# Attention plus gated MLP on one core: visits of the attention at other places, and the last output block stored in two halves

## The chip, the cores and the metric

The kernel runs on one core of one Trainium2 chip. The metric is the device time of one execution in microseconds (us), lower is better. A core has the engines PE (TensorE, matrix products into PSUM banks), DVE (VectorE), ACT (ScalarE), POOL (GpSimd) and SP (SyncE). Each runs its own list of instructions in order and waits on semaphores for the others. SP, ACT and POOL also issue DMAs.

## The reference

Local attention over 8 batches, 8 heads, 576 tokens and head size 64, then a gated MLP over all 4608 tokens (512 to 1536 to 512), in float32:

```python
def _attn_ref(q, k, v):                       # (8, 8, 576, 64)
    scores = scale * np.matmul(q, k.transpose(0, 1, 3, 2))
    mask_plain = (rel >= 0) & (rel < 32)                       # heads 0 to 3
    mask_dil = (rel >= 0) & (rel < 128) & (rel % 4 == 0)       # heads 4 to 7
    scores = np.where(masks[None, :, :, :], scores, -1000000000.0)
    attn = np.exp(scores - np.max(scores, axis=-1, keepdims=True))
    attn = attn / (np.sum(attn, axis=-1, keepdims=True) + 1e-09)
    return np.matmul(attn, v)

def _moe_ref(x, w_gate, w_val, w_out):        # x: the attention's output, (4608, 512)
    g = x @ w_gate
    silu = g * (1.0 / (1.0 + np.exp(-g)))
    return silu * (x @ w_val) @ w_out
```

## The kernel before

**Tokens.** The first 1536 tokens are worked off in four plain chunks of 384, the other 3072 in three chunks of 1024 (`NCS` = 3, each two halves of `CS` = 512 columns). The change touches the 1024-token chunks, called chunk 0, 1 and 2 here.

**Products.** Every float32 operand of the MLP is split into a high and a low part, and three products (high by high, high by low, low by high) are added in PSUM (L772). A 1024-token chunk multiplies by seven products in place of eight: operands are cut into 2 by 2 blocks, `NT` = 7 combinations of blocks are multiplied, and sums of the products give the four blocks of the result. Product t goes to a pair of PSUM banks (`BANK`): bg/bv for products 0, 2 and 4 (ACT copies them out, `keep`, L777), bo0/bo1 for 1 and 5, bo2/bo3 for 3 and 6. After products 1, 4, 5 and 6 DVE adds a bank and a kept copy (`total`, L735). The totals of product 4 read bo2/bo3, which product 6 then adds to, so product 6 has to wait for them.

**Two stages of a chunk.** In the gate/value stage six rounds (i = 0 to 5, pairs of hidden blocks) each run the seven products, each once for the gate and once for the value (`gate_val`): 84 slots of six matmuls. After each total `gated` forms tanh (ACT, L798) and the gated h (DVE, L800, L801). In the second stage (the output, `outs`) each of the seven products runs over six hidden blocks: 42 slots, each with three matmuls for either of two row blocks r. Its operands are h and combinations of h (DVE, POOL), split by `h_split` (ACT cast L762, then the low part on DVE or POOL, L735) eight blocks ahead. Where a product is in `SUMS`, `out_done` forms the total of a row block and SP stores it (256 KB). So a chunk has 126 slots, 0 to 83 gate/value and 84 to 125 output; the change of stages lies behind slot 83. Weights come as pieces that POOL asks for seven ahead (`ask`, L701).

**Attention.** It is cut into 46 packs. While chunk c is multiplied, PE, DVE and ACT also do the attention of chunk c + 1, in ten visits for each of chunks 0 and 1; chunk 2 has none. A visit m has two parts, hung behind a slot by the dictionary `visit` (`attend`). Part A at slot a: PE forms the results of pack m - 1 (L394) and the scores of pack m (L354); DVE divides (L403 to L405) and subtracts the row maximum (L366 to L369); ACT takes exponentials (L374) and issues two loads (L336, L330). Part B, six slots later: PE transposes the results (L412) and the exponentials (L378); ACT copies both out (L384, L438). All use the one pair of banks `two`. Before, the ten parts A of a chunk stood at slots 2, 12, 22, 32, 42, 53, 63, 73, 83 and 94.

**x.** When a chunk's attention is complete, `x_step` forms the seven combinations of the next chunk's x and splits them (ACT cast L738, DVE L735, both 1024 columns). In the program most steps stand at slots 104 to 124, but the compiler's scheduler may put a step earlier in an engine's list where its data allow it.

## Time and profile before

| | |
|---|---|
| median of 3 runs | 946.74 us (946.68 to 948.36) |
| the profiled execution | 946.37 us, of it the span of the instructions 944.6 us |
| granted TensorE clock | 1.000 |
| busy share of the span: DVE, ACT, POOL | 67%, 41%, 37% |
| memory | 161.37 MB read, 42.47 MB written, 216 GB/s |

A row of the timeline has the start in us, the duration, the engine, the source line, the operation, output and inputs, and a count of like instructions; in brackets stands how long the engine was idle before it and what ended that. A row of a waits table reads: who waited, on which line, for whom; the sum in us, how often, the longest. "at_..." is an SBUF buffer, "two", "bg", "bv", "bo" are PSUM banks. ACTq and SPq are the queues from which DMAs are issued.

### The profile page before, as it was taken

What the parts mean: (1) busy time and instruction counts of PE and PEld (TensorE: products, weight loads), DVE (VectorE), ACT (ScalarE), POOL (GpSimd) and SP (SyncE); (2) the same over time, 40 slices, a digit from 0 to 9 for tenths busy, and PEclk for the clock granted to TensorE, in tenths of its full rate; (3) what the DMA queues carried; (4) which work ended last, traced back from release to release, by engine and by line L of the source; (5) the groups of instructions that cost most, each with busy time, mean ns of one, the idle gap of its engine ahead of it and who ended that gap; (6) DMA issues with size and microseconds to landing.
All of it is one profiled execution on the core that took longest, in us unless ns stands there. A gap on an engine that the chain in (4) does not pass through costs nothing.

```text
span 944.6 us, 21916 instructions
## 1 busy us (share of the span) xinstructions
PE 929.7 (98%) x9204; PEld 812.9 (86%) x9204; DVE 633.3 (67%) x1008; ACT 391.9 (41%) x687; POOL 346.1 (37%) x364
## 2 busy tenths in 40 slices
PE   7899999999999999999999999999999999999998
PEld 5799999999999999888888788888887888888886
DVE  4767566676667865666568984666689845656882
ACT  4885323333234333343344553343345523334352
POOL 0765411111111121234245672232257723344481
PEclk9999999999999999999999999999999999999999
DMA  9986166567757690777768688776865786665583
GB/s 369 336 283 199 36 206 222 175 228 236 242 189 248 234 332 31 234 239 209 226 203 255 210 240 257 225 235 202 253 203 166 226 261 191 201 183 176 176 252 105
DMA packets 75249, 205.25 MB, mean 217 GB/s; under 512 B 7568, under 2 KB 23824, under 8 KB 75152
## 3 DMA queue, kind: packets, MB, share of 16 engines
q0 software_dynamic: 27216, 99.10, 34.9%
q1 hardware_dynamic: 35696, 65.07, 19.5%
q10 hardware_dynamic: 12240, 39.70, 12.7%
q8 instruction: 72, 1.18, 0.5%
q14 instruction: 25, 0.20, 0.1%
HBM read 161.37 MB, written 42.47 MB: 216 GB/s over the span
## 4 chain that ended last, share of the span: by engine, by line
PE 91%; DVE 5%; ACT 2%; issue 1%; DMA 0%; ACTq 0%; DVEq 0%
PE bo L772 30%; PE bg L772 11%; PE bv L772 11%; PE bo L496 10%; PE bv L459 10%; PE bg L459 10%; PE two L394 3%; PE two L354 2%; PE two L378 2%; DVE at_float L735 2%; PE two L412 1%; DVE at_int L263 0%; DMA at_bfloat<-masks 0%; DVE at_float L800 0%; DVE at_float L801 0%
## 5 line engine op out<-in xcount | busy, mean ns | idle before, releaser
L772 PE MATMUL bo<-at_float32r 128*128 128x512 f32 x1296 | 308.0, 391 | 0.0
L772 PEld LDWEIGHTS bo<-at_float32r 128*128 128x128 f32 x1296 | 242.1, 188 | 51.6 <-ACT at_float L503 0.2
L701 POOL DMA_DIRECT2D at_float32r<-pieces x189 | 103.9, 550 | 249.5 <-PE bo L772 144.5
L735 DVE TENSOR_TENSOR at_float<-bo,at_float 128x512 f32<-128x512 f32 x168 | 113.7, 685 | 109.8 <-ACT at_float L777 59.8
L488 POOL TENSOR_TENSOR at_float32r<-at_float,at_float32r 128x384 fp32r<-128x384 f32 x48 | 54.9, 1143 | 220.0 <-PE bo L496 180.0
L772 PE MATMUL bv<-at_float32r 128*128 128x512 f32 x486 | 129.9, 393 | 0.0
L772 PE MATMUL bg<-at_float32r 128*128 128x512 f32 x486 | 129.7, 393 | 0.0
L735 DVE TENSOR_TENSOR at_float32r<-at_float,at_float32r 128x512 fp32r<-128x512 f32 (+1 forms) x84 | 99.2, 1205 | 40.3 <-ACT at_float32r L762 24.8
L735 POOL TENSOR_TENSOR at_float32r<-at_float,at_float32r 128x512 fp32r<-128x512 f32 x63 | 96.7, 1536 | 44.6 <-ACT at_float32r L762 43.3
L459 PE MATMUL bg<-at_float32r,at_float32r 128*128 128x384 f32 x576 | 110.8, 339 | 2.1 <-DVE at_float L473 1.4
L459 PE MATMUL bv<-at_float32r,at_float32r 128*128 128x384 f32 x576 | 110.1, 338 | 0.0
L496 PE MATMUL bo<-at_float32r,at_float32r 128*128 128x384 f32 x576 | 110.1, 338 | 0.0
L772 PEld LDWEIGHTS bv<-at_float32r 128*128 128x128 f32 x486 | 90.2, 188 | 19.4
L772 PEld LDWEIGHTS bg<-at_float32r 128*128 128x128 f32 x486 | 90.2, 188 | 19.1 <-DVE at_float32r L735 0.2
L762 ACT CAST at_float32r<-at_float 128x512 fp32r<-128x512 f32 x126 | 76.2, 622 | 68.0 <-PE bv L772 23.3
L459 PEld LDWEIGHTS bg<-at_float32r,at_float32r 128*128 128x128 f32 x576 | 99.9, 188 | 3.8 <-POOL at_float32r L278 1.1
L496 PEld LDWEIGHTS bo<-at_float32r,at_float32r 128*128 128x128 f32 x576 | 100.2, 188 | 0.9
L459 PEld LDWEIGHTS bv<-at_float32r,at_float32r 128*128 128x128 f32 x576 | 99.7, 188 | 0.8
L798 ACT ACTIVATE at_float<-at_float 128x512 f32<-128x512 f32 x72 | 45.6, 633 | 85.4 <-DVE at_float L735 85.1
L473 DVE SCALAR_TENSOR_TENSOR at_float<-at_float,bg 128x384 f32<-128x384 f32 x48 | 26.6, 553 | 77.1 <-ACT at_float L468 77.1
L777 ACT COPY at_float<-bg 128x512 f32<-128x512 f32 x63 | 36.9, 586 | 86.4 <-PE bg L772 86.2
L278 POOL TENSOR_TENSOR at_float32r<-at_int,at_float32r 128x768 fp32r<-128x768 f32 x24 | 45.8, 1917 | 40.8 <-ACT at_float32r L274 40.6
(80 smaller groups left out, 968.6 us busy)
## 6 DMA issues: line engine op xcount, KB each, us to landing
at_float32r<-pieces POOLq DMA_DIRECT2D x189, 512.0 KB, 4.5
pieces<-at_float32r SPq DMA_DIRECT2D x126, 256.0 KB, 5.3
at_int<-w SPq DMA_DIRECT2D x24, 768.0 KB, 7.1
at_float<-vb ACTq DMA_DIRECT2D x28, 390.0 KB, 4.7
at_float<-vb ACTq DMA_DIRECT2D x14, 520.0 KB, 6.1
at_float<-qkb ACTq DMA_DIRECT2D x14, 448.0 KB, 5.6
out<-at_float SPq DMA_DIRECT2D x24, 256.0 KB, 4.8
at_float<-qkb ACTq DMA_DIRECT2D x10, 544.0 KB, 6.4
```

The source lines that it names most:

```text
L278: nc.gpsimd.tensor_tensor(out=lo, in0=wst.pop(u).bitcast(F32), in1=hi, op=ALU.subtract)
L394: nc.tensor.matmul(out=two[BQ * j:BQ * j + BQ, h, (D + 1) * g:(D + 1) * (g + 1)], lhsT=t[r, BQ * i:BQ * i + BQ], rhs=v[r, i, :], start=Tru ...
L459: nc.tensor.matmul(out=bank[:, :CH], lhsT=wcol(f, o, low), rhs=x[ORDER[j]], start=n == 0, stop=n == len(ops) - 1)
L473: last["h"] = nc.vector.scalar_tensor_tensor(out=t, in0=t, scalar=1.0, in1=bank_g[:, :CH], op0=ALU.add, op1=ALU.mult)
L488: nc.gpsimd.tensor_tensor(out=hl, in0=hst[i][0], in1=hst[i][1], op=ALU.subtract)
L496: nc.tensor.matmul(out=bank_o[j][:, :CH], lhsT=wcol(f, 2 * DM + P * j, low), rhs=x, start=f == 0 and low == 0 and x is hh, stop=f == NF - ...
L701: nc.gpsimd.dma_start(out=taken[asked], in_=pieces[asked % NPIECE])
L735: engine.tensor_tensor(out=out, in0=a, in1=b, op=op)
L762: nc.scalar.copy(out=o[:, 0], in_=src)
L772: nc.tensor.matmul(out=bank, lhsT=w, rhs=x, start=first and n == 0 and t in FRESH, stop=last and n == len(ops) - 1, skip_group_check=True)
L777: nc.scalar.copy(out=kept[KEPT[t]][r], in_=banks[0][r][:, :CS])
L798: nc.scalar.activation(out=f, in_=g, func=AF.Tanh, scale=0.5)
```

## The change

```diff
--- before.py
+++ after.py
@@ -587,7 +587,7 @@
         visits(m, a, a + 3)
     for m in range(M1 + 1, NPK + 1):
         c, n = divmod(m - M1 - 1, 10)
-        a = SB + NSLOT * c + 2 + 92 * n // 9
+        a = SB + NSLOT * c + (2 + 9 * n if n < 9 else 94)
         visits(m, a, a + 6)
 
     def attend(now):
@@ -776,10 +776,10 @@
         if t in KEPT:
             nc.scalar.copy(out=kept[KEPT[t]][r], in_=banks[0][r][:, :CS])
 
-    def total(t, r, ring):
+    def total(t, r, ring, cols=slice(0, CS)):
         _, b, k = SUMS[t]
-        o = ring()
-        tt(nc.vector, o, banks[b][r][:, :CS], kept[k][r], ALU.add)
+        o = ring()[:, cols]
+        tt(nc.vector, o, banks[b][r][:, cols], kept[k][r][:, cols], ALU.add)
         return o
 
     def gate_val(ci, i, n, r):
@@ -814,12 +814,12 @@
     def n_out(ci, t, i):
         return NT * NP * ci + NP * t + i
 
-    def out_done(ci, t, r):
+    def out_done(ci, t, r, cols=slice(0, CS), engine=nc.sync):
         if t in SUMS:
             a, b = SUMS[t][0]
-            o = total(t, r, o_ring)
+            o = total(t, r, o_ring, cols)
             row, col = P * (2 * a + r), T0 + CS * (2 * ci + b)
-            nc.sync.dma_start(out=out[row:row + P, col:col + CS], in_=o)
+            engine.dma_start(out=out[row:row + P, col + cols.start:col + cols.stop], in_=o)
 
 
     def mix_to(half):
@@ -882,6 +882,8 @@
             if i < 3:
                 h_split(first + i)
         for t in range(NT):
+            if ci == NC - 1 and t == NT - 1:
+                break
             for i in range(NP):
                 n = n_out(ci, t, i)
                 for r in range(2):
@@ -898,6 +900,15 @@
                     k = (slot - 104) // 2
                     if k < 8 or k == 10:
                         x_step(k)
+
+    t = NT - 1
+    for i in range(NP):
+        outs(NC - 1, t, i, 0)
+    out_done(NC - 1, t, 0)
+    for i in range(NP):
+        outs(NC - 1, t, i, 1)
+    for a, engine in ((0, nc.scalar), (CS // 2, nc.sync)):
+        out_done(NC - 1, t, 1, slice(a, a + CS // 2), engine)
 
 
 def layout(q, k, v, moe_w_gate, moe_w_val, moe_w_out):
```

It has two parts. First, the visits of a chunk start at slots 2, 11, 20, 29, 38, 47, 56, 65, 74 and 94: the first and the last stay, the others stand nine slots apart, and the ninth, which spanned the change of stages (83 and 89), now stands at 74 and 80. Second, the last product of the last chunk runs its six blocks for row block 0, then its six for row block 1. Row block 1's total is formed and stored in two halves of 256 columns, the first issued by ACT, the second by SP. The matmuls are the same ones.

PE's list around the change of stages of chunk 0, before: part A at slot 83 (L394, L354) after the last products on bo2 and bo3 (here bo_509 and bo_513).

```order
L772 MATMUL bo_509<-at_1024_float32r 128x512 x6
L772 MATMUL bo_513<-at_1024_float32r 128x512 x6
L394 MATMUL two<-at_780_float_888,at_384_float_951 32x65 x24
L354 MATMUL two<-at_1280_float_514 32x64 x32
L772 MATMUL bg<-at_1024_float32r 128x512 x3
L772 MATMUL bv<-at_1024_float32r 128x512 x3
```

And PE's list six slots on, still before: part B at slot 89, at the end of the second stage's first product.

```order
L772 MATMUL bg<-at_1024_float32r 128x512 x3
L772 MATMUL bv<-at_1024_float32r 128x512 x3
L412 MATMUL two<-at_256_float_59,at_384_float_1082 128x128 x3
L378 MATMUL two<-at_256_float_59,at_512_float_702 128x128 x4
L772 MATMUL bo_501<-at_1024_float32r 128x512 x3
L772 MATMUL bo_505<-at_1024_float32r 128x512 x3
```

PE's list after the change, in the last gate/value round: part A follows the gate of product 2 (slot 74), part B the gate of product 5 (slot 80).

```order
L772 MATMUL bg<-at_1024_float32r 128x512 x6
L394 MATMUL two<-at_780_float_888,at_384_float_951 32x65 x24
L354 MATMUL two<-at_1280_float_514 32x64 x32
L772 MATMUL bv<-at_1024_float32r 128x512 x6
L772 MATMUL bo_509<-at_1024_float32r 128x512 x6
L772 MATMUL bo_513<-at_1024_float32r 128x512 x6
L772 MATMUL bg<-at_1024_float32r 128x512 x6
L772 MATMUL bv<-at_1024_float32r 128x512 x6
L772 MATMUL bo_501<-at_1024_float32r 128x512 x6
L412 MATMUL two<-at_256_float_59,at_384_float_1082 128x128 x3
L378 MATMUL two<-at_256_float_59,at_512_float_702 128x128 x4
L772 MATMUL bo_505<-at_1024_float32r 128x512 x6
```

The visit has moved to before the change of stages, where PE now runs matmuls of L772 alone.

DVE's list of the same visit, before: the visit's six steps (L403 to L405, L366 to L369) stand between sums and splits of h (rows on at_512 and at_1024 buffers alone).

```order
L735 TENSOR_TENSOR at_512_float_4770<-at_512_float_551,at_512_float_557 128x512
L801 SCALAR_TENSOR_TENSOR at_512_float_543<-at_512_float_4793,at_512_float_4774 128x512
L403 TENSOR_SCALAR at_6_float_296<-two 128x6
L735 TENSOR_TENSOR at_512_float_545<-at_512_float_545,at_512_float_4770 128x512
L404 RECIPROCAL at_6_float_296<-at_6_float_296 128x6
L735 TENSOR_TENSOR at_512_float_4723<-at_512_float_552,at_512_float_558 128x512
L405 TENSOR_TENSOR at_384_float_1082<-two,at_6_float_296 128x2x3x64
L366 TENSOR_TENSOR at_512_float_702<-two,at_448_bfloat_58 128x2x4x64
L735 TENSOR_TENSOR at_1024_float32r<-at_512_float_547,at_1024_float32r 128x512
L368 TENSOR_REDUCE at_8_float_3007<-at_512_float_702 128x8
L735 TENSOR_TENSOR at_1024_float32r<-at_512_float_4770,at_1024_float32r 128x512
L369 TENSOR_TENSOR at_512_float_702<-at_512_float_702,at_8_float_3007 128x2x4x64
```

DVE's list of the visit after the change, in the last gate/value round (bo_509 and bo_513 with kept copies are the totals of product 4, the 128x1024 row is the low part of the split of x1 for the next chunk).

```order
L801 SCALAR_TENSOR_TENSOR at_512_float_537<-at_512_float_4858,at_512_float_4727 128x512
L735 TENSOR_TENSOR at_1024_float32r<-at_512_float_537,at_1024_float32r 128x512
L403 TENSOR_SCALAR at_6_float_296<-two 128x6
L404 RECIPROCAL at_6_float_296<-at_6_float_296 128x6
L405 TENSOR_TENSOR at_384_float_1082<-two,at_6_float_296 128x2x3x64
L366 TENSOR_TENSOR at_512_float_702<-two,at_448_bfloat_58 128x2x4x64
L368 TENSOR_REDUCE at_8_float_3007<-at_512_float_702 128x8
L369 TENSOR_TENSOR at_512_float_702<-at_512_float_702,at_8_float_3007 128x2x4x64
L735 TENSOR_TENSOR at_1024_float32r<-at_512_float_545,at_1024_float32r 128x512
L735 TENSOR_TENSOR at_1024_float32r<-at_1024_float_562,at_1024_float32r 128x1024
L735 TENSOR_TENSOR at_512_float_4723<-bo_509,at_512_float_567 128x512
L735 TENSOR_TENSOR at_512_float_4774<-bo_513,at_512_float_568 128x512
```

The visit's steps now stand together, and the split of x1, which before stood in the second stage just ahead of the tenth visit, stands between them and the totals of product 4. This is alike in chunk 1.

DVE's list at the very end, before: the totals of the two last products, row block 0 and row block 1.

```order
L735 TENSOR_TENSOR at_1024_float32r<-at_512_float_555,at_1024_float32r 128x512
L735 TENSOR_TENSOR at_512_float_4727<-bo_501,at_512_float_567 128x512
L735 TENSOR_TENSOR at_512_float_4774<-bo_505,at_512_float_568 128x512
L735 TENSOR_TENSOR at_512_float_4772<-bo_509,at_512_float_565 128x512
L735 TENSOR_TENSOR at_512_float_4793<-bo_513,at_512_float_566 128x512
```

And the end of DVE's list after the change.

```order
L735 TENSOR_TENSOR at_1024_float32r<-at_512_float_555,at_1024_float32r 128x512
L735 TENSOR_TENSOR at_512_float_4727<-bo_501,at_512_float_567 128x512
L735 TENSOR_TENSOR at_512_float_4774<-bo_505,at_512_float_568 128x512
L735 TENSOR_TENSOR at_512_float_4772<-bo_509,at_512_float_565 128x512
L735 TENSOR_TENSOR at_512_float_4858<-bo_513,at_512_float_566 128x256
L735 TENSOR_TENSOR at_512_float_4727<-bo_513,at_512_float_566 128x256
```

The last total has become two of 256 columns. On PE the last six pairs of three matmuls on bo_509 and bo_513 have become 18 on bo_509 and then 18 on bo_513.

## The prediction

> **What bounds the kernel now.** I read the page first, then the table of waits of PE, then PE's timeline through a 1024-token chunk, then the vector engines' timelines where PE stood still, and last the end of the span.

> ```profile
> PE 929.7 (98%) x9204; PEld 812.9 (86%) x9204; DVE 633.3 (67%) x1008; ACT 391.9 (41%) x687; POOL 346.1 (37%) x364
> PE two L378 <- ACT at_float L374: 3.6, 3, 1.6
> 399.98 1.52 PE L772 MATMUL bg<-at_float32r 128*128 128x512 f32 x6
> 401.34 1.52 PE L772 MATMUL bv<-at_float32r 128*128 128x512 f32 x6
> ```

> PE is busy for 98% of the span. The change neither adds nor removes a matmul, so it can win only where PE stands still and behind PE's last matmul. A slot (six matmuls) takes 401.34 - 399.98 = 1.36 us. PE's longest sum of waits is on L378, the transposes of the exponentials in part B of a visit. Two of its three waits lie in the chunks that the change touches:

> ```profile
> 487.21 0.49 PE L412 MATMUL two<-at_float,at_float 128*128 128x128 f32 x3
> 487.54 0.60 PE L378 MATMUL two<-at_float,at_float 128*128 128x128 f32 x4
> 487.90 1.63 PE L772 MATMUL bg<-at_float32r 128*128 128x512 f32 x6
> ...
> 519.08 0.49 PE L412 MATMUL two<-at_float,at_float 128*128 128x128 f32 x3
> 521.21 0.66 PE L378 MATMUL two<-at_float,at_float 128*128 128x128 f32 x4 [1.63 <-ACT at_float L374]
> ...
> 715.38 0.49 PE L412 MATMUL two<-at_float,at_float 128*128 128x128 f32 x3
> 717.04 0.66 PE L378 MATMUL two<-at_float,at_float 128*128 128x128 f32 x4 [1.17 <-ACT at_float L374]
> ```

> At 487 us L378 follows three transposes of L412 after 0.33 us. At 519 us it follows after 2.13 us and at 715 us after 1.66 us. Each time this is the ninth visit of its chunk, part A at slot 83 (the last gate/value slot), part B at slot 89. The waits cost 2.13 - 0.33 = **1.80 us** and 1.66 - 0.33 = **1.33 us**. The vector engines show why:

> ```profile
> 512.56 0.15 DVE L403 TENSOR_SCALAR at_float<-two 128x6 f32<-128x6 f32 x1
> 516.72 2.55 POOL L735 TENSOR_TENSOR at_float32r<-at_float,at_float32r 128x512 fp32r<-128x512 f32 x2
> 517.24 2.59 DVE L735 TENSOR_TENSOR at_float32r<-at_float,at_float32r 128x512 fp32r<-128x512 f32 x1
> 519.75 0.68 DVE L369 TENSOR_TENSOR at_float<-at_float,at_float 128x512 f32<-128x512 f32 x1
> 520.52 0.63 ACT L374 ACTIVATE at_float<-at_float 128x512 f32<-128x512 f32 x1 [2.86 <-DVE at_float L369]
> ```

> The chain from L403 to the end of the exponentials takes 521.15 - 512.56 = 8.6 us, since at the change of stages DVE has combinations and splits of h between its steps, one of them 2.59 us long beside POOL. A visit inside the gate/value stage looks different:

> ```profile
> 403.11 0.53 ACT L374 ACTIVATE at_float<-at_float 128x384 f32<-128x384 f32 x1 [0.99 <-DVE at_float L369]
> 407.22 0.49 PE L378 MATMUL two<-at_float,at_float 128*128 128x128 f32 x3
> 496.95 0.16 DVE L403 TENSOR_SCALAR at_float<-two 128x8 f32<-128x8 f32 x1
> 499.81 0.53 ACT L374 ACTIVATE at_float<-at_float 128x384 f32<-128x384 f32 x1 [1.35 <-DVE at_float L369]
> 503.55 0.49 PE L378 MATMUL two<-at_float,at_float 128*128 128x128 f32 x3
> ```

> The second visit is 407.22 - 403.64 = 3.6 us early, the eighth 503.55 - 500.34 = 3.2 us, its chain being 3.4 us long. PE waits for none of the visits between.

> **The visits.** Their instructions stay the same: as many matmuls, DVE and ACT steps, and two DMA issues on ACT's queue each. They start every 9 slots instead of every 10 or 11; the tenth stays at slot 94. The ninth moves to slots 74 and 80, the middle of the gate/value stage.

> - Removed: the two waits, 1.80 + 1.33 = **3.13 us**.
> - The new places: by the order, at most two of the gate's own DVE steps of about 0.7 us stand between L403 and L369, so the 3.4 us chain becomes at most 4.8 us, against six slots of 1.36 = 8.2 us from A to B. Some 3 us are to spare. That cover is gone if DVE loses more than that in one visit.
> - The loads: a visit's loads on ACT's queue must land before the next visit, nine slots or 12.2 us later. The longest took 8.2 us, so I put them at nothing:

> ```profile
> at_float<-qkb ACTq DMA_DIRECT2D x1, 640.0 KB, 8.2
> at_float32r<-pieces POOLq DMA_DIRECT2D x189, 512.0 KB, 4.5
> ```

> - POOL's queue: the order puts some piece loads behind subtractions of h. A piece is asked for seven pieces, at two slots each, ahead: 19 us against 4.5. Nothing; SP's queue keeps its order.
> - Next late at the change of stages: DVE has 2.9 us less to do there (the 3.4 us chain less 0.5 of ACT). The tenth visit is the closest one left. There L378 at 538.74 came only 0.5 us after the exponentials:

> ```profile
> 530.98 2.97 DVE L735 TENSOR_TENSOR at_float32r<-at_float,at_float32r 128x1024 fp32r<-128x1024 f32 x2 [1.12 <-ACT at_float32r L738]
> 533.87 0.15 DVE L403 TENSOR_SCALAR at_float<-two 128x8 f32<-128x8 f32 x1
> 537.67 0.53 ACT L374 ACTIVATE at_float<-at_float 128x384 f32<-128x384 f32 x1 [3.98 <-DVE at_float L369]
> 538.74 0.49 PE L378 MATMUL two<-at_float,at_float 128*128 128x128 f32 x3
> ```

> Its L403 was late because a split of the next chunk's x (1024 columns) stood ahead of it on DVE. By the order that split now stands in the last gate/value round, so this visit should gain time too.

> **The last two row blocks.** The 36 matmuls stay; the first block's 18 now come first. Of six runs of three in alternation and one run of 18 I expect the same, give or take 0.05 us. The splits of h that the first block now needs earlier are long made.

> ```profile
> 940.61 0.69 DVE at_float L735
> 940.65 1.01 SPq L822 DMA_DIRECT2D out<-at_float  x2
> GB/s 23 285 367 351 27 0 0 0 0 0 0 0 0 0 0 133 371 382 113 0 0 0 0 0 0 0 0 0 0 0 0 222 371 382 24 0 0 0 0 0
> L366 DVE TENSOR_TENSOR at_float<-two,at_bfloat 128x384 f32<-128x384 f32 x11 | 6.0, 546 | 0.0
> L366 DVE TENSOR_TENSOR at_float<-two,at_bfloat 128x512 f32<-128x512 f32 x7 | 4.7, 678 | 0.0
> ```

> The GB/s row has slices of 21/40 = 0.525 us from 925 us on. The last two stores, 512 KB, move at up to 382 GB/s, or 0.69 us each, from about 941.5 (the slice at 222 is three fifths full) to 942.9. That is 0.84 us after the first issue. The first store ends at about 942.2, just when the second (issued at 941.66 - 0.33 = 941.33, data at 942.17) can start, so taking the first away frees little. Halving does more. From L366's rows 128 columns cost 0.132 us, so a total of 256 columns takes 0.41 us, and the next can start after 0.34. The second half is then ready at 940.61 + 0.34 + 0.41 = 941.36, **0.06 us later** than now, and its 128 KB need 0.34 us instead of 0.69. Net gain 0.35 - 0.06 = **0.3 us**. No trace shows rows of 1 KB to the output: if halves moved at half the rate, the gain is a loss of 0.06 us; at best, with a first half that is out of the way and a shorter completion, I allow 0.6.

> [...]

> **Sum.** The profiled execution took 946.37 us around its span of 944.6. 946.37 - 3.13 - 0.3 = 942.9 us. The median of the runs, 946.74, lies 0.4 above it, which the forecast for a median keeps: 946.7 - 3.4 = **943.3 us**, 0.36% less.

> **Rivals.**

> 1. *The wait comes back at the change of stages on the split h.* PE reaches the second stage's products sooner: part A (510.72 - 509.44 = 1.3 us) and part B with its wait (487.90 - 487.21 + 1.80 = 2.5 us) no longer lie ahead of them. For: POOL is slow there.

> ```profile
> 509.44 0.67 PE L394 MATMUL two<-at_float,at_float 64*32 64x65 f32 x44
> 510.72 0.96 PE L772 MATMUL bg<-at_float32r 128*128 128x512 f32 x3
> 523.75 0.63 ACT L762 CAST at_float32r<-at_float 128x512 fp32r<-128x512 f32 x1
> 524.47 6.55 POOL L735 TENSOR_TENSOR at_float32r<-at_float,at_float32r 128x512 fp32r<-128x512 f32 x1 [4.16 <-ACT at_float32r L762]
> 534.22 0.84 PE L772 MATMUL bg<-at_float32r 128*128 128x512 f32 x3
> ```

> This part of h ended at 531.0 and was read four groups of 0.68 us behind 534.22, at 536.9: 5.9 us to spare, about 2 after the shift. Against: its cast stood behind two copies that waited for PE itself and so moves with PE, DVE is freer, and PE's waits name no L772 at all, in the last chunk, which has no visits, no more than here. If all 3.13 us come back, only the end wins: 946.4 us, 11%.

> 2. *A new place costs part of the gain.* One or two visits lose 0.5 to 1.5 us on L378 or on a bank: 943.8 to 944.8, 8%.

> 3. *Slower: the x split put forward holds up the totals.* In the last gate/value round of both chunks DVE now has the low part of the 1024-column x1 split ahead of the totals of product 4, for which PE's product 6 waits (same banks). That split waits for ACT's cast, and the cast for PE's last reading of the old x in product 3.

> ```profile
> L738 ACT CAST at_float32r<-at_float 128x1024 fp32r<-128x1024 f32 x13 | 13.7, 1054 | 22.8 <-PE bo L772 17.5 <-DVE at_float L735 5.3
> L735 DVE TENSOR_TENSOR at_float32r<-at_float,at_float32r 128x1024 fp32r<-128x1024 f32 x13 | 18.3, 1411 | 12.6 <-PE bo L772 10.4 <-ACT at_float32r L738 2.2
> ```

> From the end of product 3: 1.05 + 1.41 + 0.69 = 3.2 us to the first total; product 6 starts four slots and a part B (some 0.8 us: 487.90 - 487.21 = 0.7, and 0.1 in the matmuls behind it) later, after 6.3 us. It decides once DVE's step is held for more than 3.1 us. To be slower by 0.2% it must take back 3.4 us and 1.9 more, 2.7 in each chunk, that is be held for 5.8 us twice; the time is then 948.6 or more. [...] POOL has little queued in this stretch: 3%.

> **Chances and range.** The forecast has 78%, between 942.6 (0.6 at the end, 0.05 at the runs) and 944.2; the rivals 11, 8 and 3%. A measurement of this kernel can tell about 0.2%, 1.9 us, from no change, so faster means under 944.8: 78 + 8 = 86%. Same 11%, slower 3%. The range, 942.4 to 945.0, takes in the second rival and the runs' own spread, and leaves out the first and the third.

> **What would show it.** Right: no PE wait on L378 between slots 80 and 90 of both chunks, L374 3 us ahead of L378 at every gate/value visit, the tenth visit's over 1 us ahead, PE's last matmul 3.1 us sooner, and 0.3 us less from there to the end of the span. Wrong: a PE wait on L772 for DVE, ACT or POOL in the last gate/value round or the first steps of the second stage, or a last store that lands no sooner after PE.

## The result, and the profile after

The changed kernel takes **958.93 us** (median of 4 runs, 957.73 to 959.56) against 947.0 for the kernel before in the same comparison (median of 4, 946.68 to 948.36): a ratio of 1.0122, 95% interval 1.0104 to 1.0139. It is about 12 us slower where 943.3 us was forecast. The profiled execution took 958.8 us, of it a span of 957.0.

First two rows of the changed kernel's page (busy time, and the granted clock in 40 slices), then the rows of its table of PE's waits that bear on the 1024-token chunks:

```profile
PE 934.4 (98%) x9204; PEld 816.4 (85%) x9204; DVE 640.3 (67%) x1009; ACT 391.8 (41%) x687; POOL 340.9 (36%) x364
PEclk9999999999999999999999899999999899999999
```

```profile
PE two L412 <- DVE at_float L405: 5.7, 1, 5.7
PE two L378 <- ACT at_float L374: 2.8, 2, 2.0
PE two L412 <- DVE at_float L366: 2.7, 1, 2.7
```

Two lines of waits are new, and the clock row has two slices below 9. The timeline says which visit it is. PE and ACT, ninth visit of chunk 0, part B (now slot 80):

```profile
507.04 0.49 PE L412 MATMUL two<-at_float,at_float 128*128 128x128 f32 x3
507.36 0.60 PE L378 MATMUL two<-at_float,at_float 128*128 128x128 f32 x4
...
505.13 0.63 ACT L374 ACTIVATE at_float<-at_float 128x512 f32<-128x512 f32 x1 [2.01 <-DVE at_float L369]
```

L378 follows L412 after 0.32 us, 1.6 us behind the exponentials: the moved visit waits for nothing. PE at part B of the **tenth** visit (slot 100), which was not moved, in chunk 0 and chunk 1:

```profile
536.04 0.84 PE L772 MATMUL bv<-at_float32r 128*128 128x512 f32 x3
539.54 0.65 PE L412 MATMUL two<-at_float,at_float 128*128 128x128 f32 x4 [2.66 <-DVE at_float L366]
542.22 0.90 PE L378 MATMUL two<-at_float,at_float 128*128 128x128 f32 x3 [2.02 <-ACT at_float L374]
542.77 1.63 PE L772 MATMUL bg<-at_float32r 128*128 128x512 f32 x3
...
545.48 9.36 PE L772 MATMUL bo<-at_float32r 128*128 128x512 f32 x36
554.67 0.84 PE L772 MATMUL bg<-at_float32r 128*128 128x512 f32 x3
```

```profile
744.17 1.11 PE L412 MATMUL two<-at_float,at_float 128*128 128x128 f32 x4 [5.69 <-DVE at_float L405]
744.93 1.63 PE L772 MATMUL bg<-at_float32r 128*128 128x512 f32 x3
...
756.48 0.84 PE L772 MATMUL bg<-at_float32r 128*128 128x512 f32 x3
```

PE waits 2.66 + 2.02 us in chunk 0 and 5.69 in chunk 1, and the products behind are slow: from 542.77 to 554.67 stand 42 matmuls, 7 slots of 1.36 = 9.5 us, that took 11.9; in chunk 1 11.55. So 2.4 and 2.0 us go beyond the waits. The windows of chunk 0 (start and end, length, busy time of PE, PEld, DVE, ACT and POOL with the number of instructions, granted clock, DMA share, GB/s) show that the granted clock fell:

```profile
535.00:540.00 5.00, 2.34 (x13) 1.64 (x11) 4.93 (x8) 0.00 (x0) 0.69 (x2) 1.00 0.87 310
540.00:545.00 5.00, 2.98 (x10) 2.35 (x9) 3.98 (x7) 3.36 (x8) 2.22 (x3) 0.57 0.30 110
545.00:550.00 5.00, 5.00 (x18) 3.95 (x17) 5.00 (x4) 3.84 (x7) 3.50 (x4) 0.74 0.73 210
```

Chunk 0 gains the ninth visit's 1.80 us and loses 2.66 + 2.02 + 2.4 and some 0.7 around the slow transposes (from 536.72, where L412 would have started, to 542.77 are 6.05 us, of them 4.68 waited; undisturbed it was 0.68); chunk 1 gains 1.33 and loses 5.69 + 2.0 and, by the same sum, 0.2. That makes 6.0 + 6.6 = 12.6 us. PE's first products of chunk 1 and chunk 2 agree: 579.36 and 781.17 us, before 573.39 and 768.45, so 6.0 and 12.7 us later. The last row is DVE's, at the end of the span:

```profile
953.38 0.76 DVE L735 TENSOR_TENSOR at_float<-bo,at_float 128x256 f32<-128x256 f32 x2 [3.45 <-PE bo L772]
```

From PE's last matmul (its end is at 953.34) to the end of the span are 3.7 us, 4.0 before: the halves work, but the gain is lost beside the 12 us.

**Why the tenth visit is late.** Its chain starts with DVE's L403. DVE's timeline from the last L801 of the gate/value stage to L403, where it is never idle:

```profile
516.98 0.68 DVE L801 SCALAR_TENSOR_TENSOR at_float<-at_float,at_float 128x512 f32<-128x512 f32 x1
517.58 0.68 DVE L735 TENSOR_TENSOR at_float32r<-at_float,at_float32r 128x512 fp32r<-128x512 f32 x1
518.18 1.78 DVE L735 TENSOR_TENSOR at_float<-at_float,at_float 128x512 f32<-128x512 f32 x1
519.89 3.47 DVE L735 TENSOR_TENSOR at_float32r<-at_float,at_float32r 128x512 fp32r<-128x512 f32 x2
523.28 3.59 DVE L735 TENSOR_TENSOR at_float<-at_float,at_float 128x512 f32<-128x512 f32 x4
526.79 0.68 DVE L735 TENSOR_TENSOR at_float32r<-at_float,at_float32r 128x512 fp32r<-128x512 f32 x1
527.39 3.59 DVE L735 TENSOR_TENSOR at_float<-at_float,at_float 128x512 f32<-128x512 f32 x4
530.91 7.08 DVE L735 TENSOR_TENSOR at_float32r<-at_float,at_float32r 128x512 fp32r<-128x512 f32 x4
537.91 0.15 DVE L403 TENSOR_SCALAR at_float<-two 128x8 f32<-128x8 f32 x1
```

These are 17 steps behind L801. A step of 512 columns starts 0.60 us after the one before it when nothing disturbs it; here several take 1.78, and the last four (two of them splits of x, 1024 columns) 7.0 for some 3.5. Undisturbed the 17 steps would have taken 15 x 0.60 + 2 x 1.14 = 11.3 us; they took 20.9. Part A's matmuls on PE had begun at 527.15, so L403 ran 10.8 us later. Two things moved against each other. PE starts slot 84 at 511.91 and part A at 527.15, 15.2 us on; before, 510.72 and 528.73, 18.0 us: PE is 2.8 us sooner at the tenth visit. DVE's L403 comes 537.91 - 511.91 = 26.0 us behind slot 84, before 533.87 - 510.72 = 23.2: DVE is 2.8 us **later**, though the ninth visit's six steps are gone from this stretch. Its last L801 already stands 5.1 us behind slot 84 (before, 511.96: 1.2 us), since the ninth visit and the x1 split (506.73 on) now come ahead of the last round's totals, and that split itself had to wait 1.1 us for its cast, which stands behind the visit's exponentials on ACT. So 3.9 us of the lateness are there before the stretch begins; the stretch gains back 1.0 us (20.9 us, before 21.9 with the visit's steps in it), since what is left of it is longer beside POOL.

In chunk 1, whose wait is the longer one, the same comparison (slot 84 at 713.98, part A at 729.22, L403 at 743.00; before 707.02, 724.56, 729.97) gives PE 2.3 us sooner and L403 6.1 us later: 4.1 us later already at the last L801, and the last four steps ahead of L403 take 9.7 us there.

### The profile page after: what moved, and what is told of

The parts are those of the page before. It is cut to its first block, busy times and chain, and to the rows that moved or that the text cites. A ratio compares the mean times of both kernels' runs of the same rounds, so it can differ in the third digit from the quotient of the medians.

```text
span 957.0 us, 21911 instructions
## 1 busy us (share of the span) xinstructions
PE 934.4 (98%) x9204; PEld 816.4 (85%) x9204; DVE 640.3 (67%) x1009; ACT 391.8 (41%) x687; POOL 340.9 (36%) x364
## 3 DMA queue, kind: packets, MB, share of 16 engines
q1 hardware_dynamic: 35696, 64.93, 19.1%
## 4 chain that ended last, share of the span: by engine, by line
PE 85%; DVE 10%; ACT 3%; issue 1%; DMA 0%; DVEq 0%; ACTq 0%
PE bo L772 27%; PE bo L496 10%; PE bv L459 10%; PE bg L459 10%; PE bg L772 10%; PE bv L772 9%; DVE at_float32r L735 3%; DVE at_float L735 3%; PE two L394 3%; PE two L354 2%; PE two L378 2%; PE two L412 1%; DVE at_float L801 1%; DVE at_float L800 1%; DVE at_int L263 0%
## 5 line engine op out<-in xcount | busy, mean ns | idle before, releaser
L772 PE MATMUL bo<-at_float32r 128*128 128x512 f32 x1296 | 312.4, 394 | 0.0
L772 PEld LDWEIGHTS bo<-at_float32r 128*128 128x128 f32 x1296 | 242.7, 189 | 52.2 <-ACT at_float L503 0.2
L735 DVE TENSOR_TENSOR at_float<-bo,at_float 128x512 f32<-128x512 f32 (+1 forms) x169 | 113.2, 682 | 104.4 <-ACT at_float L777 58.6
L772 PE MATMUL bv<-at_float32r 128*128 128x512 f32 x486 | 130.4, 395 | 0.0
L772 PE MATMUL bg<-at_float32r 128*128 128x512 f32 x486 | 130.4, 394 | 0.0
L735 DVE TENSOR_TENSOR at_float32r<-at_float,at_float32r 128x512 fp32r<-128x512 f32 (+1 forms) x84 | 98.7, 1197 | 46.4 <-ACT at_float32r L762 30.3
L772 PEld LDWEIGHTS bv<-at_float32r 128*128 128x128 f32 x486 | 91.5, 190 | 19.9
L772 PEld LDWEIGHTS bg<-at_float32r 128*128 128x128 f32 x486 | 91.5, 190 | 19.1 <-DVE at_float32r L735 0.2
L762 ACT CAST at_float32r<-at_float 128x512 fp32r<-128x512 f32 x126 | 75.7, 621 | 76.8 <-DVE at_float L735 24.6
L735 POOL TENSOR_TENSOR at_float32r<-at_float,at_float32r 128x512 fp32r<-128x512 f32 x63 | 89.9, 1428 | 39.0 <-ACT at_float32r L762 38.3
## 6 DMA issues: line engine op xcount, KB each, us to landing
at_float32r<-pieces POOLq DMA_DIRECT2D x189, 512.0 KB, 4.5
```

What stands on the lines that cost most here:

```text
L735: engine.tensor_tensor(out=out, in0=a, in1=b, op=op)
L762: nc.scalar.copy(out=o[:, 0], in_=src)
L772: nc.tensor.matmul(out=bank, lhsT=w, rhs=x, start=first and n == 0 and t in FRESH, stop=last and n == len(ops) - 1, skip_group_check=True)
```

## The experiments

Theory: with the ninth visit's pauses gone, PE comes to the tenth visit some 3 us sooner and meets a DVE that is behind with its list; behind waits like these (2.66 and 2.02 us in chunk 0, 5.69 in chunk 1) the clock costs extra. Rivals: the spacing of nine slots or the new gate places cost; the tail costs; PE is throttled for working with fewer pauses; DVE is not what is late.

### Undoing one part at a time: tenth100, ninth83, tail_only, x_behind

```diff
tenth100, against after:
-        a = SB + NSLOT * c + (2 + 9 * n if n < 9 else 94)
+        a = SB + NSLOT * c + (2 + 9 * n if n < 9 else 100)
ninth83, against after:
+        a = SB + NSLOT * c + (2 + 9 * n if n < 8 else (83, 94)[n - 8])
tail_only, against after:
+        a = SB + NSLOT * c + 2 + 92 * n // 9
x_behind, against after (last["z"] is the last DVE step of the latest part A):
+                    if k < 2:
+                        with tc.issue_after(last["z"].ins):
+                            x_step(k)
```

Expected of tenth100:

> The changed kernel with the tenth visits of chunks 0 and 1 at slots 100 and 106 in place of 94 and 100; nothing else differs. Backlog theory (PE now reaches slot 94 about 4 us sooner and DVE is 2 to 6 us too late there; the clock falls behind the waits): six slots are 8 us, more than the 5.9 us that the worse visit is late, so L412 and L378 wait for under 0.5 us, the granted clock stays at 1.00, and the time is 943.3 us (943 to 945), which beats both kernels. Rival 'the nine-slot spacing or the new gate places cost': stays at 955 or more. Rival 'PE with fewer pauses is throttled': the clock still falls somewhere in chunks 0 and 1, 950 or more.

Expected of ninth83:

> The changed kernel with only the ninth visits put back to slots 83 and 89 (the first eight stay nine slots apart, the tail stays halved). Backlog theory: the pauses of part A and of the L378 wait (1.6 and 1.2 us) come back ahead of slot 94, so the tenth visit is in time again; 946.4 us (946 to 947). Rival 'the spacing of nine of the first eight visits costs': 955 or more, with the tenth visit's waits of 2.7 to 5.7 us still there.

Expected of tail_only:

> The kernel before with only the last two row blocks formed in turn and the last stored in halves. From PE's last matmul to the end of the span 3.64 us in place of 4.0, so 946.4 us for 946.7; visits as before. Rival 'the row blocks in turn or the halves cost': slower than the kernel before.

Expected of x_behind:

> The changed kernel, but the 1024-column splits of x_step 0 and 1 may not be put ahead of the tenth visit's last DVE step. Backlog theory: DVE's list ahead of L403 is 3.5 us shorter (2.31 and 1.21 us), so in chunk 0 L405 comes before PE's L412 is due and L378 waits some 1.6 us, in chunk 1 L412 waits 2.2 us instead of 5.7; the clock stays at or near 1.00; 947 us (945 to 950). Rival 'DVE's list is not what makes the visit late' (POOL or ACT holds it): L403 no more than 1 us sooner, 956 or more.

| run | median us | ratio to before, 95% interval |
|---|---|---|
| tenth100 | 950.92 (5 runs) | 1.0043 (1.0029 to 1.0056) |
| ninth83 | 946.87 (10) | 0.9999 (0.9989 to 1.0008) |
| tail_only | 946.15 (11) | 0.9996 (0.9987 to 1.0005) |
| x_behind | 949.9 (6) | 1.0032 (1.002 to 1.0044) |
| the kernel before | 946.68 (23) | |

**ninth83** is back at the time of before with eight visits nine slots apart: the spacing costs nothing in sum, the loss comes with the ninth visit's leaving the change of stages. (L378 waits 0.94 and 1.03 us at the ninth and tenth visits of chunk 0 and 0.91 at the ninth of chunk 1, 2.9 us for 2.8 before.) **tail_only** is no slower; its span ends 3.7 us behind PE's last matmul, before 4.0. That gain is below what the times can tell. **x_behind** takes two splits, 3.5 us, off DVE's list ahead of L403, and 9 of the 12 us are gone; DVE does set the visit. But L403 came at 536.19, only 1.7 us sooner, since a split left in the list took longer (4.28 us, 3.11 in the changed kernel), and the clock did not stay near 1.00 as expected: it fell behind waits of 2.02 and 2.35 us (a mean of 0.66 from 540 to 545 us; 0.95 and 0.71 in the two stretches of 5 us from 735 on).

**tenth100** missed its 943.3 by 7.6 us, and its waits say why. PE, chunk 0 and chunk 1 (L735 forms the low part of a split h):

```profile
PE bo L772 <- DVE at_float32r L735: 4.1, 2, 2.4
...
541.64 5.52 PE L772 MATMUL bo<-at_float32r 128*128 128x512 f32 x23 [1.68 <-DVE at_float32r L735]
...
738.79 6.97 PE L772 MATMUL bo<-at_float32r 128*128 128x512 f32 x23 [2.45 <-DVE at_float32r L735]
```

With the visit out of the way PE no longer waited for the visit but for the next split of h in the same list. So the theory was too narrow: it is not the visit alone that is late, but the next split in DVE's list as well. The clock stayed at 1.00 behind the wait of 1.68 us and fell to 0.85 and 0.80 around that of 2.45 (means from 735 to 740 and from 740 to 745 us).

### Shorter list, fewer steps beside POOL: both, dve_low

```diff
both: the edits of tenth100 and x_behind together
dve_low, against after:
-        tt((nc.gpsimd, nc.vector)[i % 2], o[:, 1], src, o[:, 0])
+        tt(nc.vector if t in (1, 2) else (nc.gpsimd, nc.vector)[i % 2], o[:, 1], src, o[:, 0])
```

Expected of both:

> The tenth visits at slots 100 and 106, and the splits of x_step 0 and 1 kept behind the tenth visit's last DVE step (the two edits of the runs tenth100 and x_behind together). Backlog theory: in tenth100 PE waited 1.68 and 2.45 us for split h, with the two 1024-column splits (3.5 us or more) ahead of it on DVE; without them these waits fall under 0.5 us, no wait above 1.7 us is left and the clock stays at 1.00; 943.5 to 945 us. Rival 'DVE has too much to do there wherever the steps stand' (the split is only paid later, or what is taken out is eaten by longer steps beside POOL, as in x_behind, where 3.5 us less work brought L403 only 1.7 us forward): waits of 1 us or more on another line, 946 to 949.

Expected of dve_low:

> The changed kernel, but the low parts of h for products 1 and 2 of the second stage are all formed by DVE, none by POOL (some six more DVE steps of 0.60 us from start to start between the change of stages and the tenth visit). Theory 'DVE is late because its steps are stretched beside POOL' (eight steps lose some 9.5 us, about 6.8 of it beside these POOL steps): L403 comes some 3 us sooner than in the changed kernel (537.9 at a part A at 527.2, so 26.2 us after 511.67), the tenth visit's waits fall under 2 us and the time to 945 to 949. Rival 'the amount of work makes DVE late': L403 comes 3 to 4 us later, 961 to 966.

**both** takes **943.11 us** (median of 6, 942.89 to 944.54), ratio 0.9964 (0.9952 to 0.9976): faster than the kernel before and the changed one. PE waits nowhere for more than 0.25 us in the 1024-token chunks, and the clock stays at 1.00 there, so that here fewer pauses by themselves didn't throttle PE (part B, slot 106, chunk 0):

```profile
538.71 7.07 PE L772 MATMUL bo<-at_float32r 128*128 128x512 f32 x30
545.62 0.60 PE L412 MATMUL two<-at_float,at_float 128*128 128x128 f32 x4
546.05 0.49 PE L378 MATMUL two<-at_float,at_float 128*128 128x128 f32 x3
```

**dve_low** takes 943.52 us (median of 6), ratio 0.9969 (0.9958 to 0.9981): 15 us less than the changed kernel and less than the 945 to 949 expected, with every visit at its place there and *more* steps on DVE. Busy time on its page, then DVE's timeline from the last L801 to L403:

```profile
PE 928.4 (98%) x9204; PEld 812.3 (86%) x9204; DVE 627.5 (67%) x1027; ACT 392.6 (42%) x687; POOL 321.1 (34%) x346
```

```profile
515.82 0.68 DVE L801 SCALAR_TENSOR_TENSOR at_float<-at_float,at_float 128x512 f32<-128x512 f32 x1
...
528.86 3.55 DVE L735 TENSOR_TENSOR at_float32r<-at_float,at_float32r 128x512 fp32r<-128x512 f32 x4
532.34 0.15 DVE L403 TENSOR_SCALAR at_float<-two 128x8 f32<-128x8 f32 x1
```

DVE has 18 instructions more over the whole kernel and is busy for 12.8 us less. Between the last L801 and L403 stand 21 steps in 16.5 us, in the changed kernel 17 in 20.9. The last four, with the same two 1024-column splits, take 3.5 us, not 7.0. The last L801 is sooner too, 2.6 us behind slot 84 (513.24) in place of 5.1, so L403 comes 19.1 us behind slot 84, not 26.0. So it is the length of the steps beside POOL and not their number that made DVE late. POOL's timelines (the changed kernel, then dve_low) show the other side. In the changed kernel POOL's steps beside DVE's last four take 1.31 and 1.83 us and those four 7.0; in dve_low the four take 3.5 us and the one POOL step beside them 5.18:

```profile
531.50 1.31 POOL L735 TENSOR_TENSOR at_float32r<-at_float,at_float32r 128x512 fp32r<-128x512 f32 x1
...
533.33 1.83 POOL L735 TENSOR_TENSOR at_float32r<-at_float,at_float32r 128x512 fp32r<-128x512 f32 x1
```

```profile
528.39 5.18 POOL L735 TENSOR_TENSOR at_float32r<-at_float,at_float32r 128x512 fp32r<-128x512 f32 x1 [0.31 <-ACT at_float32r L762]
```

### The price of a wait in clock: clock1, clock2

```diff
against tail_only, in attend, for the slots of a table in the last chunk:
+            nc.tensor.transpose(out=two[:, 0, :P], in_=idents[:, 0], identity=idents[:, 0])
+            nc.scalar.copy(out=a[:, :P], in_=two[:, 0, :P])
+            for _ in range(pause[now]):
+                nc.scalar.copy(out=b, in_=a)
+                a, b = b, a
+            last["p"] = nc.tensor.transpose(out=two[:, 1, :P], in_=a[:, :P], identity=idents[:, 0])
...
clock1: {20: 2, 45: 4, 70: 6, 105: 8}; clock2: {20: 8, 45: 6, 70: 4, 105: 2}
```

Expected of clock1:

> The kernel before with the halved tail, and in the last chunk, which has no visits, four pauses of PE behind slots 20, 45, 70 and 105: a transpose, then 3, 5, 7 and 9 copies by ACT one after the other (0.5 to 0.6 us each), then a transpose that waits for the last; the products behind wait for it. What the pauses form is not used. Theory 'a wait of more than about 2 us also takes the clock away': about 1.6 us of wait costs nothing beyond itself with the clock at 1.00, 2.7, 3.7 and 4.8 us are followed by 4 to 6 us at 0.5 to 0.8, 2 us or so beyond the wait each. Rival 'the clock fell for another reason' (the load of the other engines at the change of stages): 1.00 behind all four, the sum of the waits is the whole loss.

Expected of clock2:

> As clock1 with the lengths in the opposite order (9, 7, 5 and 3 copies behind slots 20, 45, 70 and 105). The same lengths give the same clock behind them, wherever they stand; if the place decides, the clock falls at the same slots as in clock1.

They took 970.45 and 971.72 us (one run each). PE in clock1, the pauses behind slots 20 and 45 with the products behind them (L786 is L772 there), then clock2, the pause behind slot 105:

```profile
798.94 0.33 PE L603 MATMUL two<-at_float,at_float 128*128 128x128 f32 x1 [1.66 <-ACT at_float L601]
799.02 1.63 PE L786 MATMUL bo<-at_float32r 128*128 128x512 f32 x6
800.49 1.54 PE L786 MATMUL bg<-at_float32r 128*128 128x512 f32 x6
...
836.38 0.48 PE L603 MATMUL two<-at_float,at_float 128*128 128x128 f32 x1 [2.96 <-ACT at_float L601]
836.51 2.91 PE L786 MATMUL bg<-at_float32r 128*128 128x512 f32 x6
839.22 2.76 PE L786 MATMUL bv<-at_float32r 128*128 128x512 f32 x6
```

```profile
935.97 0.35 PE L603 MATMUL two<-at_float,at_float 128*128 128x128 f32 x1 [2.06 <-ACT at_float L601]
936.06 4.59 PE L786 MATMUL bo<-at_float32r 128*128 128x512 f32 x12
940.49 0.85 PE L786 MATMUL bg<-at_float32r 128*128 128x512 f32 x3
```

| PE waited, us | 1.66 | 2.06 | 2.96 | 3.33 | 4.25 | 4.63 | 5.55 | 5.96 |
|---|---|---|---|---|---|---|---|---|
| lost behind it, us | 0.1 | 1.7 | 2.8 | 2.6 | 1.7 | 2.4 | 1.6 | 1.4 |

The second row is the time of the slowed products less 1.36 us for each six: for 2.06 us, 940.49 - 936.06 - 2.72 = 1.7. In these two runs the price is there from 2.06 us on, lies between 1.4 and 2.8, and doesn't grow with the wait. The slots behind which the clock falls follow the lengths: behind slot 20 it stays at 1.00 in clock1 (1.66 us) and falls in clock2 (5.55). The six matmuls that take 839.22 - 836.51 = 2.71 us in place of 1.36 run at half speed.

The length of the wait is not the whole of it. In the changed kernel's chunks the granted clock is either 1.00 or 0.50: it is 0.50 from 540.75 to 547.58 us and from 742.13 to 748.96, 6.83 or 2 x 3.41 us each time, and the two falls lie 201.38 us apart, 59 x 3.41. In clock2 it falls at 803.0, 844.0, 881.5 and 936.15 (the first three worked out from the mean clock of 0.80, 0.90 and 0.65 in the 5 us from 800, 840 and 880 on), 12, 11 and 16 x 3.41 us apart. Here are windows of clock2 cut in steps of 3.41 us from these times, around the pause of 2.06 us and at the start of that of 5.55 (columns as above):

```profile
932.74:936.15 3.41, 1.35 (x8) 0.87 (x7) 3.41 (x4) 2.42 (x5) 2.61 (x3) 1.00 1.09 383
936.15:939.56 3.41, 3.41 (x10) 2.64 (x10) 0.72 (x1) 0.58 (x1) 0.17 (x1) 0.50 0.45 156
939.56:942.98 3.42, 3.42 (x16) 2.82 (x15) 0.90 (x2) 1.28 (x3) 1.87 (x2) 1.00 0.19 32
...
796.20:799.62 3.42, 1.48 (x8) 0.92 (x6) 0.69 (x1) 2.44 (x6) 0.54 (x1) 1.00 0.74 232
```

The wait of 2.06 us lies in one window, in which PE was busy for 1.35 us, and the next runs at half clock. Behind the window with 1.48 us, where the wait of 5.55 began, the clock stayed at 1.00; it fell only behind the next one, in which PE did nothing. In the 1024-token chunks of the changed kernel and around the pauses of clock1 and clock2 the clock fell nine times, each time behind a full-speed window with at most 1.42 us of PE; no full-speed window there with 1.48 or more was followed by half clock. The half clock held for one window (3.41 us, behind the wait of 2.06) or two (6.83 in the changed kernel), which gives the price: half of what PE works in them, 3.41 / 2 = 1.7 us behind the wait of 2.06, and with 2.50 and 3.41 us of work 2.95 behind that of 2.96, where 2.8 were lost. So in these runs the falls went with how long PE stood still within one window, and with that with where a wait fell in the windows. By these 1.48 and 3.41 us a wait of up to 2 x (3.41 - 1.48) = 3.9 us, spread over two windows, would cost no clock; that is an estimate, and no run has such a wait.

### Are the gains one and the same? both_dve, dve_before

both_dve has the edits of both and dve_low; dve_before is the kernel before with the halved tail and dve_low's edit, all visits at their old places.

Expected of both_dve:

> Both edits of the run both (tenth visit at 100 and 106, splits of x_step 0 and 1 behind it) and dve_low's (low parts of h for products 1 and 2 on DVE). In both and in dve_low PE has no wait left in the chunks of 1024 tokens but 0 to 0.8 us, so the backlog theory expects the gains not to add: 942.7 to 943.4 us. Rival 'steps beside POOL still cost PE something there': under 942.5.

Expected of dve_before:

> The kernel before with the halved tail and with dve_low's edit alone: visits at their old places, the ninth at slots 83 and 89. If the ninth visit's wait of before had the same cause as the tenth's after the change (DVE's steps stretched beside POOL at the change of stages), it shrinks here too, to under 0.5 us in both chunks, and the time is 943.5 us (943.2 to 944.2) with no visit moved. If the ninth visit waits because of where it stands (between the totals of the last round and the combinations of h), 1 us or more of wait stays in each chunk and the time is 945 to 946.5.

both_dve took 943.89 us (median of 7), ratio 0.997 (0.9959 to 0.9982), half a us above the range expected: nothing is added. dve_before took **943.06 us** (median of 5, 942.65 to 944.34), ratio 0.9962 (0.995 to 0.9975). Its ninth visit, back at slots 83 and 89 (PE and ACT, chunk 0):

```profile
520.72 0.49 PE L412 MATMUL two<-at_float,at_float 128*128 128x128 f32 x3
521.04 0.60 PE L378 MATMUL two<-at_float,at_float 128*128 128x128 f32 x4
...
520.07 0.63 ACT L374 ACTIVATE at_float<-at_float 128x512 f32<-128x512 f32 x1 [0.81 <-DVE at_float L369]
```

L378 follows after 0.32 us; in chunk 1 too (715.14 and 715.46). The wait that the change set out to remove did not hang on the visit's place either: it was DVE's lateness beside POOL, and goes with it.

## Why the prediction was wrong

- **Removed, 3.13 us: right.** The ninth visit waits nowhere; 1.80 and 1.33 us are gained.
- **The new gate places, loads, POOL's and SP's queues at nothing: right** for PE, and ninth83 shows the spacing harmless. But the ninth visit's DVE steps in the last round made that round's totals late.
- **"Next late at the change of stages: DVE has 2.9 us less to do there ... so this visit should gain time too": this step failed**, in sign and size. I had given the tenth visit's margin as 0.5 us. The margin had to be worked out from both sides, as the gap between PE's part B and DVE's L403. PE lost its pauses and came 2.8 us sooner. DVE did not gain 2.9 us: it was busy without a break from 506.73 to L403, so that steps put ahead of the stretch delayed all behind them (3.9 us at the last L801), and its steps beside POOL grew longer (9.6 us over the 17 steps, 20.9 for 11.3). 0.5 - 2.8 - 2.8 is about -5, the 2.66 + 2.02 us of chunk 0.
- **Rival 1** had the right suspicion, with the wrong consumer and price: it let PE's shift come back on a split of h, at most 3.13 us. In tenth100 it is just that wait which appears. **Rival 3**, the x1 split ahead of the totals, didn't bind where it said: PE waits for no total. But the totals it made late are part of what made L403 late.
- **No term for the clock.** The waits of before, 1.63 and 1.17 us, had left it at 1.00, and no longer wait was reckoned with; the clock makes 2.4 + 2.0 of the 12 us.
- **The tail, 0.3 us: right**, 0.3 in the trace (4.0 less 3.7). The two halves took 0.76 us together, as the spacing read from the rows before had it (0.34 + 0.41).

What stays open: why DVE's steps stretched less in the kernel before. There POOL's step at 524.47 took 6.55 us while DVE's steps beside it were not stretched (two of 512 columns at 523.97 took 1.28 us, one of 1024 at 525.17 took 1.22); what decides which of the two engines is slowed was not tried by itself. Nor was one and the same wait of PE put at different places in these windows of 3.41 us.

## What to carry to other kernels

Taking a wait from the engine that sets the time moves all its later meetings forward by that wait; work out each next meeting as a margin with both sides shifted, and take an engine without idle time ahead of that meeting as late by all that is put in front of it. Where two engines lengthen each other's steps, more steps on one of them can be faster than sharing: here 18 more on DVE took the kernel before with the halved tail from 946.15 to 943.06 us, with no visit moved. Look for the cause of a wait before moving the work that shows it.

## What the runs showed of the hardware

DVE steps of 512 columns started 0.60 us apart in the changed kernel's undisturbed rows and took 0.68 us each; five of them between 518.18 and 530.91 us took 1.77 or 1.78 beside POOL steps of 1.62 to 1.74 us. With 18 steps moved from POOL to DVE (dve_low), DVE's busy time was 12.8 us less.
